# Block-sparse attention and a gated feed-forward layer on one core: four weight slices loaded and converted in halves, all operations in another order

## The chip, the cores and the metric

The kernel runs on one core of one Trainium2 chip. The metric is the time of one execution on the device in microseconds (us). PE is TensorE (matrix products), DVE is VectorE, ACT is ScalarE, POOL is GpSimd and SP is SyncE, which here issues nearly all loads and stores. Each engine has one queue of instructions and works through it in order.

## The reference

The inputs are q, k and v (4 batches, 8 heads, 768 positions, 64 wide) and two weight matrices, w_in (512 x 2048) and w_out (2048 x 512), all float32. Attention is local and blockwise, and its result goes through a layer with a cosine gate.

```python
def _attn_ref(q, k, v):
    B, H, S, D = q.shape
    block, window = (32, 16)
    nb = S // block
    k_sum = k.reshape(B, H, nb, block, D).max(axis=3)
    v_sum = v.reshape(B, H, nb, block, D).mean(axis=3)
    scores_l = scale * np.matmul(q, k.transpose(0, 1, 3, 2))
    mask_l = np.abs(pos[:, None] - pos[None, :]) < window
    scores_s = scale * np.einsum('bhsd,bhnd->bhsn', q, k_sum) + np.log(block)
    scores_l_m = np.where(mask_l, scores_l, -1000000000.0)
    a = softmax(np.concatenate([scores_l_m, scores_s], axis=-1))
    return np.matmul(a, np.concatenate([v, v_sum], axis=2))

def _moe_ref(x, w_in, w_out):
    h = x @ w_in
    return (h * np.cos(h)) @ w_out
```

The attention's output, heads side by side, is x (3072 x 512).

## The kernel before, in words

The 3072 rows of x are cut into eight blocks of 384 rows (half a batch each). A block has four groups, a to d, of two heads. a0 is group a of block 0, d7 group d of block 7. For each group the kernel loads q, k and v, turns q and k so that the head's width lies on the partitions, takes the maxima of k over blocks of 32, makes the scores, the exponentials and the normalized weights, turns those, and multiplies by v and the block means of v. The group's 128 columns of x are kept as a high part and a low part (xh, xl), so that products in a faster format lose nothing.

The feed-forward layer is cut into 16 slices of 128 columns of w_in and 128 rows of w_out. w0 to w15 are the slices. A step is one block with one slice. There are 128 of them, s0 to s127: s0 to s5 are block 0 with slices 0 to 5, s6 to s21 block 1 with all 16, s22 to s31 block 0 with slices 6 to 15, and from s32 on each block has 16. A step is twelve products that make h (`up`, L738), five operations on ACT, DVE or POOL that make the gate and its two parts (`tu`, `re`, `si`, `ga`, `hi`, `lo`: L748, L751, L756, L760, L383 or L385, L389), and nine products that add to the block's output (`dh` and `dl`, L789).

A slice is loaded by two DMAs (L404 for w_in, L408 for w_out), shifted by some bytes. ACT takes a byte of each element apart (`ab`, L417) and makes bits of it (`sh`, L422); DVE joins them with the rest (`fb`, L429); the result is split into a high part (`hi`, L383 on ACT or L385 on DVE) and a low part (`lo`, L389). Each of these handles 128 x 1024 elements: 512 columns of w_in's part and 512 of w_out's.

The order of everything is written out by hand in ORDER (L32), a text of tokens such as `w1.ab.1` (slice 1, operation ab, into buffer 1) or `s1.up.0` (step 1, the up products, into PSUM bank 0). The last letter of a token may name the engine: a is ACT, v is DVE, p is POOL. The program emits instructions in this order, so each engine's queue, and SP's queue of DMAs, has the order of the tokens that belong to it; semaphores follow from the data. FILL (L22) names tokens ahead of which PE is given products of zeros (L960), and how many. The tokens of attention are q, k, v and m (loads at L468, L468, L489 with L497, and L504; m brings the block means to where the group reads them), tk and tq (turns on PE, L532 and L519), ck and cq (copies, L383 or L385 and L525 or L527), ks (maxima, L551), ms (masks as a product, L571), sc (scores, L593), mx (L610), ex (L626), sm (L635), iv (L638), nm (POOL, L641), tp (turns, L650), cp (copies), va (the product with the values, L694), xh and xl (L383 or L385, L389). For batch 0 the block means of v come from `v0_0` and `v0_1`: l is the load (L906), vm six products (L914), ve the copies. For later batches POOL or DVE sums v (`v1_0` to `v3_7`, `s`, L254).

## Time and profile before

| what | value |
|---|---|
| three runs | 634.01, 634.37, 636.49 us (median 634.37) |
| the profiled execution | 635.47 us, its span 633.6 us |
| granted clock of TensorE, mean | 1.00 |
| PE busy | 620.6 us |
| DVE busy | 426.8 us |
| ACT busy | 315.7 us |
| POOL busy | 208.7 us |
| HBM read and written | 54.43 MB and 16.52 MB |

The span is the time from the first to the last instruction. An engine's busy time is the sum of its instructions' times, overlaps counted once. A row in order of time has the start, the length, the engine, the line, what is written and read, the shape and the count; the brackets behind it give how long the engine had been idle ahead of it and what ended that. A row with a count above one is merged from instructions that follow each other, and its length is that of all of them.

### The profile page before, as it was taken

The page shows a single profiled execution, that of the slowest core. Times are in us where ns is not written, and L with a number is a line of the kernel's source. Part 1 is how long each engine was busy: PE and PEld are TensorE (multiplying, and loading weights), DVE is VectorE, ACT ScalarE, POOL GpSimd, SP SyncE. Part 2 cuts the span into 40 slices and gives each one's busy share as a digit, 9 for nine tenths or more (in the row PEclk, how much of TensorE's full clock was granted, in tenths as well). Part 3 has the DMA queues.
Part 4 walks back from the last instruction along what each step waited for, and adds up shares of the span by engine and source line. Part 5 has one row for each costly group of instructions (what it writes and reads, how often), then busy time and mean ns, then how long its engine had stood idle before and what let it go on. Part 6 is the DMA issues. An engine that isn't in the chain of part 4 may idle for free.

```text
span 633.6 us, 12128 instructions
## 1 busy us (share of the span) xinstructions
PE 620.6 (98%) x4596; PEld 546.6 (86%) x4596; DVE 426.8 (67%) x795; ACT 315.7 (50%) x557; POOL 208.7 (33%) x243
## 2 busy tenths in 40 slices
...
GB/s 218 289 235 203 283 238 187 164 80 109 104 157 123 100 152 117 110 87 115 77 128 98 134 109 109 72 78 62 72 116 87 100 47 98 93 25 34 17 1 50
DMA packets 171305, 74.10 MB, mean 117 GB/s; under 512 B 136944, under 2 KB 160112, under 8 KB 171248
## 3 DMA queue, kind: packets, MB, share of 16 engines
...
q10 hardware_dynamic: 144, 0.13, 0.1%
HBM read 54.43 MB, written 16.52 MB: 112 GB/s over the span
## 4 chain that ended last, share of the span: by engine, by line
PE 91%; SPq 3%; DVE 2%; DMA 2%; ACT 1%; POOL 0%; issue 0%; DVEq 0%; ACTq 0%
PE banks L738 41%; PE banks L789 41%; PE banks L694 4%; PE banks L581 3%; DMA late<-in_moe_w_out_dram 2%; SPq L468 2%; PE banks L650 1%; PE banks L593 0%; ACT L756 0%; SPq L497 0%; SPq L906 0%; SPq L489 0%; ACT t L756 0%; DVE t L760 0%; DVE xl L389 0%
## 5 line engine op out<-in xcount | busy, mean ns | idle before, releaser
L738 PE MATMUL banks<-xh,w 128*128 128x384 f32 x1024 | 267.0, 337 | 0.0
L789 PE MATMUL banks<-w,gh 128*128 128x512 f32 x768 | 197.4, 392 | 0.6 <-DVE stage L827 0.6
L738 PEld LDWEIGHTS banks<-xh,w 128*128 128x128 f32 x1024 | 185.3, 188 | 2.4 <-issue 1.3
L738 PE MATMUL banks<-xl,w 128*128 128x384 f32 x512 | 171.1, 334 | 0.0
L789 PEld LDWEIGHTS banks<-w,gh 128*128 128x128 f32 x768 | 142.7, 188 | 31.4 <-issue 1.2
L389 POOL TENSOR_TENSOR gl<-t,gh 128x384 fp32r<-128x384 f32 x67 | 68.7, 1029 | 240.2 <-DVE gh L385 84.6
L748 ACT ACTIVATE t<-banks 128x384 int32<-128x384 f32 x128 | 62.3, 489 | 162.4 <-PE banks L738 88.0
L751 DVE SCALAR_TENSOR_TENSOR t<-t,banks 128x384 f32<-128x384 int32 x128 | 69.7, 547 | 66.7 <-ACT t L748 66.3
L789 PE MATMUL banks<-w,gl 128*128 128x512 f32 x384 | 108.7, 391 | 0.0
L760 DVE TENSOR_TENSOR t<-t,banks 128x384 f32<-128x384 f32 x128 | 69.6, 548 | 41.9 <-ACT t L756 40.2
L756 ACT ACTIVATE t<-t 128x384 f32<-128x384 f32 x128 | 66.3, 523 | 63.0 <-DVE t L751 62.7
L738 PEld LDWEIGHTS banks<-xl,w 128*128 128x128 f32 x512 | 96.1, 188 | 0.3
L789 PEld LDWEIGHTS banks<-w,gl 128*128 128x128 f32 x384 | 71.8, 188 | 15.3 <-issue 0.2
L641 POOL TENSOR_TENSOR sc<-sc,r 128x720 f32<-128x720 f32 x28 | 40.1, 1432 | 58.6 <-DVE r L638 54.5
L383 ACT CAST gh<-t 128x384 fp32r<-128x384 f32 x62 | 31.4, 510 | 35.3 <-DVE t L760 19.2
L617 POOL TENSOR_TENSOR sc<-sc,m 128x720 f32<-128x720 f32 x24 | 34.0, 1415 | 44.5 <-DVE m L614 41.3
L389 DVE TENSOR_TENSOR gl<-t,gh 128x384 fp32r<-128x384 f32 x61 | 38.9, 640 | 11.5 <-ACT gh L383 6.6
L385 DVE CAST gh<-t 128x384 fp32r<-128x384 f32 x66 | 25.3, 383 | 15.8 <-PE banks L789 12.5
L254 POOL TENSOR_TENSOR kn<-kn 96x256 f32<-96x256 f32 (+1 forms) x38 | 25.7, 677 | 23.7 <-DMA kn<-in_v_dram 22.0
L601 DVE SCALAR_TENSOR_TENSOR sc<-banks,mask 128x360 f32<-128x360 f32 x48 | 24.2, 519 | 13.4 <-PE banks L581 13.4
L635 DVE TENSOR_REDUCE r<-sc 128x6 f32<-128x726 f32 x28 | 25.1, 897 | 10.0 <-ACT sc L631 9.6
L664 DVE STREAM_TRANSPOSE stage<-sc 128x768 f32<-128x768 f32 x24 | 23.3, 970 | 10.5 <-POOL sc L641 10.2
(115 smaller groups left out, 558.0 us busy)
## 6 DMA issues: line engine op xcount, KB each, us to landing
pd<-stage SPq DMA_DIRECT2D x24, 384.0 KB
late<-in_moe_w_out_dram SPq DMA_DIRECT2D x16, 511.6 KB
late<-in_moe_w_in_dram SPq DMA_DIRECT2D x16, 510.5 KB
pt<-pd SPq DMA_DIRECT2D x72, 96.0 KB
vn<-in_v_dram SPq DMA_DIRECT2D x50, 120.0 KB
...
kn<-in_v_dram SPq DMA_DIRECT2D x24, 192.0 KB
...
```

Source lines behind the costliest of these rows:

```text
L254: eng.tensor_tensor(out=t[:, :n], in0=t[:, :n], in1=t[:, n:], op=ALU.add)
L383: eng.copy(out=out, in_=in_)
L389: eng.tensor_tensor(out=lo, in0=src, in1=hi.bitcast(F32), op=ALU.subtract)
L617: nc.gpsimd.tensor_tensor(out=self.sc, in0=self.sc, in1=self.m.unsqueeze(2).broadcast_to([P, U, NK]), op=ALU.subtract)
L641: nc.gpsimd.tensor_tensor(out=self.sc, in0=self.sc, in1=self.r.unsqueeze(2).broadcast_to([P, U, NK]), op=ALU.mult)
L694: nc.tensor.matmul(out=self.xps[rows, t * QT : (t + 1) * QT], lhsT=self.vn[:, t, rows], rhs=self.pt[2 * c + hh][s], start=True, stop=True,)
L738: nc.tensor.matmul(out=self.h, lhsT=w_of(name, self.f)[:, c * P : (c + 1) * P], rhs=x_of(self.blk, part, c), start=n == 0, stop=n == last,)
L748: nc.scalar.activation(out=self.t.bitcast(I32), in_=self.h, func=AF.Copy, scale=1.0 / TWO_PI, bias=0.25)
L751: nc.vector.scalar_tensor_tensor(out=self.t, in0=self.t.bitcast(I32), scalar=-TWO_PI, in1=self.h, op0=ALU.mult, op1=ALU.add)
L756: nc.scalar.activation(out=self.t, in_=self.t, func=AF.Sin, scale=-1.0, bias=-0.5 * math.pi)
L760: nc.vector.tensor_tensor(out=self.t, in0=self.t, in1=self.h, op=ALU.mult)
L789: nc.tensor.matmul(out=self.acc[i], lhsT=g[:, i * P : (i + 1) * P], rhs=w_of(name, self.f), start=self.first and n == 0, stop=self.last an ...
```

## The change

Slices 1, 0, 2 and 5 are loaded and converted in two halves. Half 0 is w_in's part, half 1 is w_out's. A token such as `w1.l.0` loads one half, and `ab`, `sh`, `fb`, `hi` and `lo` take the half as a first argument; the other twelve slices go on whole. The conversion's class gets a dictionary of its pieces for this. ORDER is another text: nearly every operation of the whole program stands at another place, with other PSUM banks, and some operations are on other engines (low parts of steps are 57 times on POOL, where before has 67, and 71 times on DVE, where before has 61). The last tokens, from s127.dl on, are as before. FILL has 66 products of zeros, where before has 56, at other tokens. The diff, with ORDER cut to its first part:

```diff
-FILL = {"a0.tk.1": 15, "a0.tk.0": 2, "b0.tq": 8, "c0.tk.0": 2, "b0.tk.0": 2, "d0.tk.0": 2, "b0.tk.1": 3, "c0.tp.0": 9, "b1.ms": 4, "b1.tq": 3, "a1.ms": 3, "a0.va": 3}
+FILL = {"a0.tk.1": 18, "a0.tq": 5, "b0.tk.0": 8, "c0.tq": 5, "d0.tk.1": 3, "d0.ms": 10, "b1.ms": 5, "a0.va": 12}
...
 ORDER = """
-a0.k a0.tk.1.0 a0.ck.1.a a0.ks.1 a0.ms.7.6 a0.tk.0.5 a0.ck.0.a b0.q a0.q a0.tq.4 a0.cq.v a0.ks.0 a0.sc b0.tq.0 c0.k
-c0.tk.0.1 a0.mx a0.ex d0.k b0.k b0.tk.0.2 b0.ck.0.a c0.ks.0 d0.tk.0.3 d0.tk.1.4 d0.ck.1.v c0.tk.1.5 c0.ck.1.a
-c0.ck.0.a b0.ms.6.7 b0.tk.1.1 b0.ks.0 a0.sm d0.ks.1 a0.iv a0.nm v0_0.l c0.q c0.tq.2 c0.cq.a d0.q d0.tq.4 c0.ks.1
-c0.ms.5.2 c0.sc b0.ks.1 b0.ck.1.a b0.cq.v b0.sc d0.cq.v c0.mx w1.l a0.tp.1.0 a0.tp.0.1 w1.ab.1 w1.sh c0.ex a0.cp.1.a
-w1.fb d0.ck.0.v c0.sm w1.hi.v d0.ks.0 w1.lo.v v0_0.vm.4 v0_1.l v0_1.vm v0_1.ve.a c0.iv b0.mx a0.cp.0.v d0.ms.0.5 d0.sc
-d0.mx c0.v w0.l w0.ab.1 w0.sh w0.fb w0.hi.v w0.lo.v b0.ex a0.v c0.nm c0.tp.0.4 b1.ms.1.2 b1.q b1.tq.3 a1.ms.6.7
-b1.cq.a c0.tp.1.3 b1.sc d0.ex d0.sm d0.iv b0.sm w2.l w2.ab.1 w2.sh w2.fb w2.hi.v b0.iv a0.m c0.m a0.va.0 c0.cp.0.a
-c0.cp.1.a d0.m a1.q a0.xh.a a1.tq.5 a1.cq.a d0.nm d0.tp.1.4 c0.va.3 c0.xh.a d0.tp.0.5 d0.cp.0.a w2.lo.v w5.l w5.ab.1
-d0.cp.1.a w5.sh a0.xl c0.xl a1.sc a1.mx a1.ex c1.ms.5.0 c1.q c1.tq.3 c1.cq.v b0.nm b0.tp.0.4 w5.fb d0.v d0.va.3
-b0.cp.0.a c1.sc d1.q d1.tq.6 d0.xh.a d1.cq.a d1.ms.4.7 b0.tp.1.6 b0.cp.1.a d1.sc a1.sm a1.iv c1.mx c1.ex a1.nm b0.m
-d0.xl b1.mx b0.v b0.va.3 b0.xh.a b0.xl w5.hi.v w5.lo.p b1.ex a1.tp.1.6 a1.tp.0.5 a1.cp.1.a c1.sm b1.sm c1.iv s1.up.0
-s1.tu a1.cp.0.v s1.re d1.mx w4.l w4.ab.0 w4.sh w4.fb w4.hi.v w4.lo.v s0.up.1 s0.tu s2.up.2 s5.up.3 w3.l w3.ab.1 w3.sh
...
+a0.k a0.tk.1.0 a0.ks.1 a0.ck.1.a b0.q a0.q a0.tk.0.7 a0.tq.6 a0.cq.a a0.ks.0 a0.ms.0.1 a0.ck.0.v a0.sc c0.k b0.k
+b0.tk.0.2 b0.tq.3 b0.tk.1.4 c0.tk.1.5 w1.l.0 c0.q d0.k c0.tk.0.6 b0.ck.1.a c0.ck.1.a c0.tq.7 c0.ck.0.a w1.ab.0.1
+c0.cq.a a0.mx b0.ks.0 v0_0.l v0_1.l b0.cq.a a0.ex w1.sh.0 c0.ks.1 b0.ks.1 b0.ck.0.v c0.ms.5.4 d0.tk.1.7 c0.ks.0 c0.sc
+c0.mx c0.ex d0.tk.0.6 b0.ms.0.1 b0.sc v0_0.vm.2 w1.fb.0 a0.sm d0.ck.0.v a0.iv w1.hi.0.v w1.lo.0.p c0.sm b0.mx c0.iv
+w1.l.1 w1.ab.1.1 w1.sh.1 w1.fb.1 w1.hi.1.v b0.ex w1.lo.1.v v0_1.vm v0_1.ve.a b1.q d0.q b1.tq.5 d0.tq.4 d0.ms.3.0
+d0.ks.0 d0.ck.1.v d0.cq.v d0.ks.1 w0.l.0 w0.ab.0.1 w0.sh.0 w0.fb.0 w0.hi.0.v w0.lo.0.v w0.l.1 w0.ab.1.1 w0.sh.1 c0.v
+d0.sc b1.cq.a d0.mx d0.ex w0.fb.1 w0.hi.1.v w0.lo.1.v c0.nm a0.nm a0.tp.1.7 a0.tp.0.6 c0.tp.1.1 c0.tp.0.2 b1.ms.4.5
+b1.sc d0.sm a1.ms.0.3 w2.l.0 w2.ab.0.1 w2.sh.0 w2.fb.0 w2.hi.0.v a0.cp.0.a a0.cp.1.a c1.q a0.v d0.iv d0.nm w2.lo.0.v
+w2.l.1 w2.ab.1.1 a0.m a0.va.6 c0.cp.1.a c0.cp.0.a b0.sm b0.iv a1.q a1.tq.7 a1.cq.v a0.xh.a a0.xl w2.sh.1 w2.fb.1
+c1.tq.1 d0.tp.1.2 a1.sc c1.cq.a c0.m c0.va.6 d0.cp.1.a a1.mx a1.ex d0.tp.0.7 d0.cp.0.a c1.ms.1.2 c1.sc b0.nm w2.hi.1.v
+w5.l.0 w2.lo.1.p w5.ab.0.1 c0.xh.v c0.xl b0.tp.1.6 d0.v d1.q d1.tq.0 d1.cq.a b0.m d0.m d0.va.3 w5.sh.0 b0.cp.1.a
+b0.tp.0.7 b0.cp.0.a d1.ms.0.6 a1.sm c1.mx c1.ex b1.mx b1.ex w5.fb.0 w5.hi.0.v b0.v b0.va.7 b0.xh.v b0.xl a1.iv d1.sc
+w5.l.1 w5.lo.0.p w5.ab.1.1 w5.sh.1 d0.xh.v d0.xl s1.up.1 a1.nm a1.tp.0.7 a1.tp.1.2 s1.tu a1.cp.0.a a1.cp.1.a w4.l
+w4.ab.0 w4.sh s5.up.5 s0.up.7 s2.up.2 c1.sm w5.fb.1 c1.iv c1.nm c1.tp.1.3 c1.tp.0.4 b1.sm s1.re w5.hi.1.v d1.mx b1.iv
+d1.ex w4.fb w4.hi.v w4.lo.v w3.l w5.lo.1.p w3.ab.1 s0.tu s0.re w3.sh w3.fb w3.hi.v w3.lo.v a1.m a1.v a1.va.0 c1.cp.1.a
+c1.cp.0.a s4.up.6 s0.si s0.ga s1.si s1.ga s0.hi.a s0.lo.v v1_0.l c1.v d1.m c1.m c1.va.3 c1.xh.a c1.xl s1.hi.a s2.tu
+s3.up.4 s1.lo.v a1.xh.a s3.tu d1.sm s2.re s3.re s2.si s2.ga s0.dh.7.1.3 s2.hi.v s0.dl s1.dh s1.dl s2.dh d1.iv s3.si
+s3.ga s3.hi.a s3.lo.v s4.tu s2.lo.v s2.dl b1.nm v1_0.s.p v1_1.l v1_1.s.p w8.l d1.v b1.m s4.re d1.nm d1.tp.0.2
...


         def __init__(self, f, raw):
-            self.f, self.raw = f, raw.bitcast(I32)
-
-        def load(self):
+            self.f, self.raw, self.u = f, raw.bitcast(I32), {}
+
+        def span(self, *h):
+            return slice(h[0] * DM, (h[0] + 1) * DM) if h else slice(0, 2 * DM)
+
+        def load(self, *h):
             f, t, n = self.f, self.raw.bitcast(U8), 8 * P
-            nc.sync.dma_start(
-                out=t[:, : NC * n].rearrange("p (c n) -> p c n", c=NC)[:, :, : n - CUT],
-                in_=w_in8.rearrange("(c p) n -> p c n", p=P)[:, :, n * f + CUT : n * (f + 1)],
+            if h != (1,):
+                nc.sync.dma_start(
+                    out=t[:, : NC * n].rearrange("p (c n) -> p c n", c=NC)[:, :, : n - CUT],
+                    in_=w_in8.rearrange("(c p) n -> p c n", p=P)[:, :, n * f + CUT : n * (f + 1)],
+                )
+            if h != (0,):
+                nc.sync.dma_start(
+                    out=t[:, NC * n : 2 * NC * n - CUT], in_=w_out8[f * P : (f + 1) * P, CUT :]
+                )
+
+        def apart(self, *args):
+            *h, i = args
+            self.u[tuple(h)] = room_for(i)[:, self.span(*h)]
+            byte = self.raw.bitcast(I8).rearrange("p (n b) -> p n b", b=8)[:, self.span(*h), 4]
+            nc.scalar.activation(
+                out=self.u[tuple(h)].bitcast(F32), in_=byte, func=AF.Prelu, scale=1.0, bias=EDGE, alpha=STEEP
             )
-            nc.sync.dma_start(
-                out=t[:, NC * n : 2 * NC * n - CUT], in_=w_out8[f * P : (f + 1) * P, CUT :]
-            )
-
-
-
-        def apart(self, i):
-            self.u = room_for(i)
-            byte = self.raw.bitcast(I8).rearrange("p (n b) -> p n b", b=8)[:, :, 4]
+
+        def first_bits(self, *h):
             nc.scalar.activation(
-                out=self.u.bitcast(F32), in_=byte, func=AF.Prelu, scale=1.0, bias=EDGE, alpha=STEEP
-            )
-
-        def first_bits(self):
-            nc.scalar.activation(
-                out=self.u, in_=self.u.bitcast(F32), func=AF.Prelu, scale=2.0 ** 27, bias=-(2.0 ** 28) * EDGE,
+                out=self.u[h], in_=self.u[h].bitcast(F32), func=AF.Prelu, scale=2.0 ** 27, bias=-(2.0 ** 28) * EDGE,
                 alpha=1.0 / STEEP,
             )

-        def join(self):
-            rest = self.raw.rearrange("p (n two) -> p n two", two=2)[:, :, 0]
+        def join(self, *h):
+            rest = self.raw.rearrange("p (n two) -> p n two", two=2)[:, self.span(*h), 0]
             nc.vector.scalar_tensor_tensor(
-                out=self.u, in0=rest, scalar=5, in1=self.u, op0=ALU.logical_shift_right, op1=ALU.bitwise_or,
+                out=self.u[h], in0=rest, scalar=5, in1=self.u[h], op0=ALU.logical_shift_right, op1=ALU.bitwise_or,
             )
-            self.uf = self.u.bitcast(F32)
-
-        def high_part(self, eng):
-            wm[self.f] = wp.tile([P, 4 * DM], F32R, name=f"w{self.f}", tag=f"w{self.f}")
-            copy(eng, wm[self.f][:, : 2 * DM], self.uf)
-
-        def low_part(self, eng):
-            rest(eng, wm[self.f][:, 2 * DM :], self.uf, wm[self.f][:, : 2 * DM])
+
+        def high_part(self, *args):
+            *h, eng = args
+            if self.f not in wm:
+                wm[self.f] = wp.tile([P, 4 * DM], F32R, name=f"w{self.f}", tag=f"w{self.f}")
+            copy(eng, wm[self.f][:, self.span(*h)], self.u[tuple(h)].bitcast(F32))
+
+        def low_part(self, *args):
+            *h, eng = args
+            low = wm[self.f][:, 2 * DM :][:, self.span(*h)]
+            rest(eng, low, self.u[tuple(h)].bitcast(F32), wm[self.f][:, self.span(*h)])


     class Group:

```

More of the change, by code (lines that the diff above doesn't have):

```diff
@@ new lines @@
+s58.ga s58.hi.v s58.lo.v s62.tu s62.re s58.dh s58.dl s60.hi.a s59.dh s59.dl s62.si s60.lo.p s61.tu s61.re s62.ga
+s61.si s61.ga s61.hi.v c4.po a5.pt.0 c5.q c4.pi c4.va.1 b5.sc.2.6 s61.lo.p s63.tu c4.xh.v s60.dh s60.dl s63.re
+s62.hi.v c5.qt b5.z.0.v s63.si s63.ga s62.lo.v b5.z.1.v s61.dh s61.dl s63.hi.a s62.dh s62.dl s63.lo.p s63.dh s63.dl
+d4.po v3_7.l d4.pi d4.v c5.kw.a c5.sc.2.3 c4.xl d4.m d4.va.1 d4.xh.a d4.xl v3_7.s.v s65.up.6 s65.tu s65.re s65.si
+b5.mx c5.z.1.v s65.ga d5.q a5.po b5.su s63.ta.0.0.a b5.ex b5.sm s65.hi.v a6.k a6.kt.0 a6.kt.1 b5.iv s65.lo.p d5.qt
@@ new lines @@
+d5.mx c5.iv s73.up.5 s71.up.3 s72.up.0 s69.hi.a s73.tu s73.re s69.lo.p s71.tu s71.re s71.si s69.dh b5.po b5.v c6.k
+b5.m c5.nm c5.pt.1 d5.su s71.ga s73.si s73.ga a6.qt b6.ks.0 a6.kw.v s71.hi.v s69.dl s70.dh s71.lo.p s70.dl s71.dh
+s71.dl c6.kt.0 a6.sc.1.3 a6.z.0.v d5.ex d5.sm d5.iv b6.kw.a s72.tu s73.hi.a s73.lo.p d5.nm b5.pi b5.va.5 b5.xh.a
+a5.xh.v a6.z.1.v a6.mx a5.xl s72.re b6.q s75.up.1 s74.up.3 c5.po d5.pt.1 s72.si s72.ga b5.xl s76.up.6 s77.up.0 c5.v
+c5.pi c5.m c5.va.5 b6.qt s72.hi.v s72.dh c6.kt.1 s72.lo.v s72.dl s76.tu s76.re s73.dh s73.dl s76.si s74.tu s74.re
```

237 lines of the change are left out of this document (112 added, 125 removed).

## Prediction

> **What bounds the kernel now.** I read the page first, then a table of stretches, then the order in time of the first 48 us.
>
> ```profile
> span 633.6 us, 12128 instructions
> PE 620.6 (98%) x4596; PEld 546.6 (86%) x4596; DVE 426.8 (67%) x795; ACT 315.7 (50%) x557; POOL 208.7 (33%) x243
> PE 91%; SPq 3%; DVE 2%; DMA 2%; ACT 1%; POOL 0%; issue 0%; DVEq 0%; ACTq 0%
> ...
> 0.00:7.66 7.66, 5.63 (x28) 3.78 (x29) 4.15 (x22) 2.25 (x3) 5.44 (x37) 1.00 0.79 178
> 7.66:34.04 26.38, 22.34 (x343) 15.06 (x344) 17.87 (x31) 14.66 (x40) 2.78 (x2) 1.00 0.99 270
> 34.04:47.47 13.43, 11.57 (x271) 9.10 (x271) 11.85 (x20) 11.68 (x29) 5.11 (x3) 1.00 0.83 242
> 47.47:160.00 112.53, 112.53 (x740) 101.61 (x739) 96.44 (x159) 76.24 (x128) 56.83 (x57) 1.00 0.64 181
> 160.00:200.00 40.00, 39.30 (x311) 33.82 (x310) 27.98 (x53) 17.10 (x28) 17.85 (x24) 1.00 0.48 126
> 200.00:618.00 418.00, 418.00 (x2862) 374.33 (x2861) 261.85 (x502) 188.83 (x321) 120.50 (x122) 1.00 0.34 87
> 618.00:633.60 15.60, 11.20 (x50) 8.94 (x48) 6.61 (x13) 4.95 (x10) 0.20 (x1) 0.99 0.14 50
> ```
>
> The columns of the stretches are the bounds, the length, the busy time of PE, its weight loads, DVE, ACT and POOL, then the granted clock, the DMA share and GB/s. PE has work for 620.6 of 633.6 us. Its 13 us of rest are 2.03 + 4.04 + 1.86 before 47.47 us, 0.70 between 160 and 200, and 4.40 at the end, where the last step drains; the order of the last tokens is the same in both kernels. The work of PE that counts is also the same: the same products, the same 128 steps. So only two things can move: PE's rest with the products of zeros that fill it, nearly all before 47.47 us, and new rest later, where there is now almost none. DMA is 99% busy from 7.66 to 34.04: the start is held by loads.
>
> **How large the prize is.** The fills are 56 products of zeros before and 66 after.
>
> ```profile
> 1.05 3.38 PE L960 MATMUL banks<-part_sum 128*128 128x256 bf16 x15 [1.05 <-DVE part_sum L279]
> 4.38 0.88 PE L532 MATMUL banks<-ident,late 128*128 128x128 f32 x3
> 27.51 1.16 PE L960 MATMUL banks<-part_sum 128*128 128x256 bf16 x9
> 28.51 0.60 PE L650 MATMUL banks<-ident,late 128*120 128x128 f32 x4
> 46.87 0.87 PE L650 MATMUL banks<-ident,sc 128*120 128x128 f32 x6
> 47.50 0.42 PE L738 MATMUL banks<-xh,w 128*128 128x384 f32 x1
> ```
>
> The first 15 take 3.38 us, 0.225 us each, at a PE not yet at speed; nine later ones take 28.51 - 27.51 = 1.00 us, 0.11 each. Fills cost 3.38 + 41 x 0.11 = 7.9 us before and 18 x 0.225 + 48 x 0.11 = 9.3 us after, as far as they don't lie in waits. The first product of the steps (s1.up, L738) starts at 47.50. In the new order the six turns of a1 (L650, 47.50 - 46.87 = 0.63 us) come behind s1.up instead of ahead of it; all else that precedes it is the same set. So the mark to beat is 47.47 - 0.63 = 46.84. Real work ahead of that mark is 39.54 busy - 7.9 - 0.63 = 31.0 us. The new order therefore can't reach s1.up before 1.05 + 9.3 + 31.0 = 41.4: the gain is at most 5.5 us, and only with PE never waiting.
>
> **Loads.** What lands when?
>
> ```profile
> late<-in_moe_w_in_dram SPq DMA_DIRECT2D x8, 510.5 KB
> late<-in_moe_w_out_dram SPq DMA_DIRECT2D x7, 511.6 KB
> late<-in_v_dram SPq DMA_DIRECT2D x4, 384.0 KB
> late<-in_q_dram SPq DMA_DIRECT2D x12, 96.0 KB
> late<-in_v_dram SPq DMA_DIRECT2D x8, 120.0 KB
> late<-in_k_dram SPq DMA_DIRECT2D x4, 192.0 KB
> late<-in_v_dram SPq DMA_DIRECT2D x4, 40.0 KB
> ...
> 13.74 0.96 SPq L408 DMA_DIRECT2D late<-in_moe_w_out_dram  x1
> 18.95 1.14 ACT L417 ACTIVATE stage<-late 128x1024 f32<-128x1024 int8 x1 [2.18 <-DMA late<-in_moe_w_out_dram]
> 23.42 2.73 PE L914 MATMUL banks<-late,early 128*24 128x512 f32 x6 [1.21 <-DMA late<-in_v_dram]
> 27.85 1.15 ACT L417 ACTIVATE stage<-late 128x1024 f32<-128x1024 int8 x1 [0.93 <-DMA late<-in_moe_w_out_dram]
> ```
>
> A k (two issues) is 0.384 MB, a q 0.192, half of the v for the block means 0.768, a group's v 0.28, a slice 1.022, half a slice 0.511. Up to w1 the queue of before holds 4.09 MB, which landed at 18.95; up to the second v0 4.86 MB, at 23.4; up to w0 6.16 MB, at 27.85. That is near 245 GB/s from about 2 us on, plus one to two us. By that, estimated from these three rows, the new order has w1.0 (2.05 MB) at 12, v0_1 (4.16) at 20, w1.1 (4.67) at 22, w0.0 (5.57) at 25, w0.1 (6.08) at 27, w2.0 (6.87) at 30, w2.1 (7.85) at 34, the means of a0 (a0.m, 7.9, issued behind w2.1) at 34, b0's v (9.6) at 40.5, where before had 10.1 MB ahead of the end of b0's v, since w5 was loaded whole ahead of it. So the halves bring the x inputs forward by 0.5 MB, about 2 us, and nothing more: SP's queue stays in order, and the bytes are the same.
>
> **The walk.**
>
> ```profile
> 26.50 1.09 PE L593 MATMUL banks<-kd,late 64*64 64x96 f32 x48
> 29.38 0.47 PE L571 MATMUL banks<-band,turned 98*128 98x360 bf16 x2
> 34.04 0.92 PE L694 MATMUL banks<-pt,vn 120*64 120x64 f32 x24
> 36.30 0.44 PE L650 MATMUL banks<-ident,late 128*120 128x128 f32 x2 [0.87 <-DMA late<-in_moe_w_out_dram]
> 46.02 0.92 PE L694 MATMUL banks<-pt,early 120*64 120x64 f32 x24
> ...
> 29.99 1.60 ACT L626 ACTIVATE sc<-banks,m 128x120 f32<-128x120 f32 x6
> 34.86 1.39 POOL L641 TENSOR_TENSOR late<-late,r 128x720 f32<-128x720 f32 x1 [7.32 <-DVE r L638]
> 21.20 1.23 DVE L429 SCALAR_TENSOR_TENSOR stage<-late,stage 128x1024 int32<-128x1024 int32 x1 [0.99 <-ACT stage L422]
> 23.62 0.68 DVE L385 CAST w<-stage 128x1024 fp32r<-128x1024 f32 x1
> 24.69 1.21 DVE L389 TENSOR_TENSOR w<-stage,w 128x1024 fp32r<-128x1024 f32 x1
> 45.20 0.55 DVE L389 TENSOR_TENSOR xl<-banks,xh 128x384 fp32r<-128x384 f32 x1
> ```
>
> First the start. Three more cold fills (0.7 us) and five more in front of a0's q delay the first turns, but a0.sc waits for q and its copies and stays near 7.7 us: nothing, covered by the q load.
>
> Then the way to the first product with the values, a0.va, which before has at 34.04. It needs a0.m, w2.1 being just ahead of it in SP's queue: about 34 again. On the way there is a new head-of-line wait: DVE has w1.fb.1, w1.hi.1 and w1.lo.1 ahead of d0.ks.0, d0.ck.1 and d0.cq, and w1.fb.1 needs w1.1 (22) and two passes on ACT, half of 1.14 each (23.2). DVE then does about 0.6 + 0.4 + 0.6, half of the rows at 21.20, 23.62 and 24.69, and four operations of the shape of the row at 45.20 (0.55) for d0, so d0.sc starts at about 27, and PE rests up to 2 us just behind its ten fills. From there PE has two scores (27.51 - 26.50 = 1.0 each), twelve turns (1.3), two sets of masks (up to 0.47 each) and 17 fills (1.9): 6 us, ready at 33. Loads and PE nearly meet there. Value taken for a0.va: 34.0, between 32.5 (d0.sc not held up) and 36 (w1.1 and a0.m 2 us later).
>
> Then the way from a0.va to s1.up. The set of PE operations is that of before less a1's turns. Before needed 13.43 us, of which 1.86 was rest: the longest, 0.87 at 36.30, is put down to a DMA, but the row of POOL's normalizing (34.86 + 1.39 = 36.25) is what ended it, since ACT had held d0's exponential behind whole slices. Without rest 11.57 - 0.63 = 10.9 us. In the new order d0.nm comes earlier in the list, but b0.cp and with it b0.va stand on ACT behind a1.ex (1.60), w5.ab.0, d1.cq and w5.sh.0; worked along ACT from a1.mx at 38 (1.6, then eight copies and half passes of 0.4 to 0.6), b0.va starts at 42.9 and s1.up, with 0.85 and d1's 1.0 between, at 44.8. Extra hand-offs of halves: I take 0.4. So 45.2, a gain of 46.84 - 45.2 = 1.6 us. Bounds: -0.5 (a0.va at 36) to +3.3 (a0.va at 32.5 and no rest).
>
> What the halving itself costs lies in this too. One DVE row gives 1.21 us for 1024 elements, another 0.55 for 384: 1.03 ns per element and 0.15 us that each instruction pays anyhow, 22% of a half's 0.68. Nine more instructions on DVE (four joins, four high parts, one low part) make 1.4 us, 1.1 of it ahead of s1.up, where DVE rests 47.47 - 4.15 - 17.87 - 11.85 = 13.6 us. It counts only through the waits above; a third of it is the 0.4. [...]
>
> Last what follows s1.up.
>
> ```profile
> 47.47:60.00 12.53, 12.53 (x95) 12.25 (x94) 12.11 (x16) 10.61 (x22) 7.49 (x5) 1.00 0.74 195
> ```
>
> Between 47.47 and 160 PE has no rest, with DVE busy for 96.44 of 112.53. The new list of DVE from s1.up to the first step of the next block has 45 instructions where before has 38 (b0.sm and c1.sm slip past, s2, s4 and s5 have their high parts on DVE). Walked along, DVE hands over s0, s2 and the last xl with 0 to 1 us to spare. I take 0.7 us of new rest, bounds -0.7 (the rest at 160 goes too) to +4. From 200 us on the order is another, with the same kinds of operations and DVE at 63%: nothing, bounds 0 to 1.5.
>
> **Sum.** -1.6 + 0.7 = -0.9 us: a span of 632.7. The profiled execution took 635.47, 1.87 more than its span, and 1.1 more than the median of 634.37; the difference is carried to the median: 633.5.
>
> **The rivals.**
> DVE takes over behind s1.up (slower). The place: s5, w9 and the last xl. b1.xl and d1.xl, which s7.up needs, are queued on DVE behind w9.fb and w9.hi; w9's load stands in SP's queue behind a load that waits for POOL's sums. My walk has w9 landing near 66 and s7.up due at 77, and DVE with 1 us to spare. Each microsecond that DVE's list is longer than that is a microsecond of PE; from 5 us on it is slower by over 0.5%. It would be 634.37 - 1.6 + 5.5 = 638.3. For: DVE at 12.11 of 12.53 between 47 and 60 us and 18% more instructions. Against: 112 us without any rest of PE so far.
> The change doesn't do what it says. Loads come by bytes; the half of w1 lands with nobody needing it, DVE's wait for w1.1 costs 2 us ahead of d0.sc, a0.va comes at 35.6, and the gain is gone: 634.4. For: 99% DMA up to 34 us. Against: b0's v is ahead of half of w5.
> The start is free of waits (faster). Here a0.va comes at 32.5, with no rest to s1.up: -3.3 and the 0.7 us at 160 gone: 630.4. Against it: PE would have to run nearly dense from 8 us on, where before rested for 4.04 of 26.4.
> [...]
>
> **How the numbers follow.** About 0.5% (3.2 us: 631.2 and 637.5) is what a measurement of this kernel can tell from no change. Forecast 0.52 (632 to 635), no gain 0.20, free start 0.14, DVE 0.09, clock 0.05. Faster takes most of the free start, 0.13; slower the DVE rival and little of the clock, 0.10; the rest, 0.77, is the same. The range leaves out the far ends of the free start and of DVE: 630.8 to 636.6.
>
> **What would show it.** Right: a0.va near 34, s1.up between 44.5 and 46, rest ahead of d0.sc with DVE's kd copy or L429 as its end, w1.lo.1 done only after 24. Wrong: s1.up before 43.5 or after 47; more than 2 us of PE rest between s1.up and 160; any granted clock under 1.00 ahead of 40 us; rest of PE over 1.5 us between 200 and 618.

## The result, and the profile after

The changed kernel takes 642.45 us (median of 4 runs, 639.69 to 643.5) where the kernel before, on the same chip, takes 635.0 (634.01 to 636.49): a ratio of 1.0113, 95% interval 1.0083 to 1.0143. It is slower, by 1.1%. The forecast was no change, 633.5 us, and its range ended at 636.6. The profiled execution took 642.63 us, its span 640.9.

First three lines of the page of the changed kernel, then a table of stretches with the columns as before: bounds, length, busy time of PE, weight loads, DVE, ACT and POOL, granted clock, DMA share, GB/s.

```profile
span 640.9 us, 12178 instructions
PE 624.6 (97%) x4606; PEld 547.4 (85%) x4606; DVE 430.4 (67%) x813; ACT 318.0 (50%) x565; POOL 205.7 (32%) x237
PE 84%; DVE 5%; ACT 5%; issue 2%; DMA 2%; SPq 2%; POOL 0%; DVEq 0%; POOLq 0%; ACTq 0%
```

```profile
10.00:20.00 10.00, 6.49 (x129) 5.26 (x128) 6.93 (x14) 6.31 (x19) 1.09 (x1) 1.00 1.06 307
20.00:30.00 10.00, 10.00 (x69) 3.98 (x71) 6.30 (x12) 4.72 (x14) 3.40 (x3) 0.83 0.92 251
30.00:40.00 10.00, 7.95 (x139) 6.10 (x130) 8.10 (x16) 7.26 (x18) 2.83 (x2) 1.00 0.90 234
40.00:48.55 8.55, 8.30 (x234) 6.97 (x233) 7.91 (x16) 7.43 (x24) 2.21 (x3) 1.00 1.00 316
48.55:60.00 11.45, 11.45 (x96) 11.12 (x89) 11.19 (x18) 10.16 (x23) 9.54 (x8) 1.00 0.36 83
60.00:160.00 100.00, 95.86 (x576) 83.54 (x575) 82.93 (x130) 61.37 (x95) 50.95 (x52) 1.00 0.63 172
160.00:200.00 40.00, 40.00 (x317) 34.98 (x316) 31.30 (x62) 25.23 (x42) 18.86 (x25) 1.00 0.51 142
200.00:618.00 418.00, 418.00 (x2902) 373.97 (x2901) 262.33 (x514) 186.31 (x318) 109.35 (x110) 1.00 0.34 88
```

Two stretches lose the time. One is the start. s1.up (its first product) comes at 48.58 us instead of 47.50. Since the 0.63 us of a1's turns now stand behind it, that is 1.7 us behind the mark of the prediction. The other is 60 to 160 us, where PE rests 100 - 95.86 = 4.14 us; before, it had no rest from 47.47 to 160 and 0.70 us behind that. From 160 to 618 PE never rests. Measured to the last product of all (636.17 after, 628.81 before), the loss is 7.36 us: 1.08 up to s1.up and 6.29 behind it, 0.63 of which are the turns. Of the other 5.7 us, 3.4 are more rest of PE (4.14 against 0.70). For the remaining 2.2 us PE is busy longer with the same products: 583.5 us from s1.up on with the turns, 580.6 before without them. What makes it so, no run here settles.

**The start.** PE's rows in order of time, with the idle time ahead of them and what ended it in the brackets, and then ACT's:

```profile
19.91 0.32 PE L603 MATMUL banks<-kd,late 64*64 64x96 f32 x3 [2.58 <-issue]
20.16 7.03 PE L924 MATMUL banks<-late,early 128*24 128x512 f32 x12
...
29.32 1.09 PE L603 MATMUL banks<-kd,late 64*64 64x96 f32 x48
...
32.89 0.70 PE L970 MATMUL banks<-part_sum 128*128 128x256 bf16 x5 [1.03 <-ACT late L535]
...
36.27 1.47 PE L970 MATMUL banks<-part_sum 128*128 128x256 bf16 x12 [0.93 <-ACT pt L386]
37.67 0.92 PE L704 MATMUL banks<-pt,vn 120*64 120x64 f32 x24
```

```profile
31.12 0.69 ACT L424 ACTIVATE stage<-late 128x512 f32<-128x512 int8 x1 [1.95 <-DVE w L392]
...
37.69 0.70 ACT L424 ACTIVATE stage<-late 128x512 f32<-128x512 int8 x1 [1.20 <-DVE w L392]
```

At 17.3 us PE stops in the middle of b0.sc, three of its products short, for 2.58 us, and "issue" says that it waited for nothing that the profile shows. Then the twelve products for the block means take 7.03 us, where before two groups of six took about 2.7 us each. Later ACT rests twice ahead of `ab`, the byte of a slice's second half, until DVE has finished the low part of the first half. These are the second halves of w0 and w2, which use the stage buffer of their first halves. What ACT has behind the first of them comes late for PE: b1.cq (L535), which ends PE's rest at 32.89, and further on a0.cp (L386). ACT's second rest ends at 37.69, when a0.va has begun, and so doesn't hold it. a0.va is at 37.67, 3.7 us later than predicted.

**The clock.** Two stretches of 3.41 us from the same kernel: the one that holds the rest, and the next.

```profile
17.50:20.91 3.41, 1.00 (x5) 0.44 (x5) 3.21 (x8) 0.26 (x2) 1.27 (x1) 1.00 1.10 312
20.91:24.32 3.41, 3.41 (x5) 0.65 (x4) 1.95 (x2) 2.80 (x8) 3.23 (x2) 0.50 0.97 309
```

The clock is 0.50 from 20.91 to 24.32 us, right behind a stretch in which PE was busy for 1.00 of 3.41 us. In e1_buffers below, at full clock, the twelve products take 5.33 us instead of 7.03: the half clock costs 1.7 us.

**Behind s1.up.** Two of the rests, each with the rows of POOL, DVE and PE that belong to it:

```profile
70.72 1.64 POOL L257 TENSOR_TENSOR kn<-kn 96x256 f32<-96x256 f32 x2
70.16 1.89 DVE L392 TENSOR_TENSOR gl<-t,gh 128x384 fp32r<-128x384 f32 x2 [0.64 <-ACT gh L386]
72.10 0.97 PE L799 MATMUL banks<-w,gl 128*128 128x512 f32 x3 [1.37 <-DVE gl L392]
...
115.04 2.40 POOL L392 TENSOR_TENSOR w<-stage,w 128x1024 fp32r<-128x1024 f32 x1 [4.30 <-ACT w L386]
115.50 2.36 DVE L392 TENSOR_TENSOR gl<-t,gh 128x384 fp32r<-128x384 f32 x1 [1.61 <-PE banks L799]
121.32 1.66 PE L799 MATMUL banks<-w,gh 128*128 128x512 f32 x6 [1.83 <-ACT gh L386]
```

The low part of a step (`lo`, tile gl) takes DVE about 0.55 us. At 115.50 it took 2.36 and ended 0.42 us behind POOL's low part of w10, which had begun 0.46 us earlier. So it took 1.8 us longer than usual and was done only behind POOL's: these two rows read as DVE held by POOL, and in e2_lo_dve below, with w10's low part off POOL, it takes 0.56 us again. The other rest shown, at 70 us, is longer in this execution than in others: e1_shift, e1_less_fill, e1_buffers and e2_lo_dve below have the same order there and 0.44 to 0.46 us in place of 1.37.

### The profile page after: what moved, and what is told of

Same layout as the page of the kernel before. It is cut to its first block, busy times and chain, and to the rows that moved or that the text cites. A ratio compares the mean times of both kernels' runs of the same rounds, so it can differ in the third digit from the quotient of the medians.

```text
span 640.9 us, 12178 instructions
## 1 busy us (share of the span) xinstructions
PE 624.6 (97%) x4606; PEld 547.4 (85%) x4606; DVE 430.4 (67%) x813; ACT 318.0 (50%) x565; POOL 205.7 (32%) x237
## 4 chain that ended last, share of the span: by engine, by line
PE 84%; DVE 5%; ACT 5%; issue 2%; DMA 2%; SPq 2%; POOL 0%; DVEq 0%; POOLq 0%; ACTq 0%
PE banks L799 37%; PE banks L748 37%; PE banks L704 4%; PE banks L591 3%; DVE stage L436 1%; ACT stage L424 1%; ACT stage L429 1%; PE banks L924 1%; DVE w L392 1%; SPq L478 1%; DVE w L388 1%; DMA late<-in_q_dram 1%; PE banks L603 1%; DMA vn<-vs 1%; DVE t L770 0%
## 5 line engine op out<-in xcount | busy, mean ns | idle before, releaser
L392 POOL TENSOR_TENSOR gl<-t,gh 128x384 fp32r<-128x384 f32 x57 | 59.1, 1037 | 253.8 <-PE banks L799 124.7
L392 DVE TENSOR_TENSOR gl<-t,gh 128x384 fp32r<-128x384 f32 x71 | 45.1, 637 | 15.1 <-ACT gh L386 6.7
L386 ACT CAST gh<-t 128x384 fp32r<-128x384 f32 x60 | 30.5, 512 | 40.1 <-DVE t L770 22.6
L388 DVE CAST gh<-t 128x384 fp32r<-128x384 f32 x68 | 27.1, 398 | 21.6 <-PE banks L799 19.3
L257 POOL TENSOR_TENSOR kn<-kn 96x256 f32<-96x256 f32 (+1 forms) x38 | 28.8, 757 | 25.2 <-DMA kn<-in_v_dram 23.6
```

The costliest lines, as they stand in the source:

```text
L257: eng.tensor_tensor(out=t[:, :n], in0=t[:, :n], in1=t[:, n:], op=ALU.add)
L386: eng.copy(out=out, in_=in_)
L388: eng.tensor_copy(out=out, in_=in_)
L392: eng.tensor_tensor(out=lo, in0=src, in1=hi.bitcast(F32), op=ALU.subtract)
```

## The experiments

The theories were these. For the start: PE waits for its own instructions, which come by DMA behind the loads, and the clock falls after that; the shared stage buffer delays ACT. The rival: the halving itself, with more and smaller operations, costs the time. For the stretch behind s1.up: DVE is held by POOL; the rival: the new order feeds the steps too late, whatever POOL does; a second rival: the new start leaves work undone that comes due later. In the table "to the end" is from s1.up's first product to the last product of the kernel, which leaves out the final stores (from the last product to the end of the span it is 4.7 us in the changed kernel and 5.9 in e2_halves_before). The ratios are to the kernel before as timed together with each run.

| run | median us | ratio to before, 95% interval | a0.va | s1.up | to the end | half clock ahead of 160 us |
|---|---|---|---|---|---|---|
| before (five times; profile) | 634.7 to 635.5 | 1 | 34.04 | 47.50 | 581.31 | none |
| after | 642.45 | 1.0113 [1.0083, 1.0143] | 37.67 | 48.58 | 587.60 | 3.41 us at 20.9 |
| e1_shift | 639.68 | 1.0063 [1.0036, 1.0091] | 35.74 | 46.64 | 586.45 | 3.41 at 28.8 |
| e1_less_fill | 643.6 | 1.0137 [1.0097, 1.0177] | 34.39 | 48.46 | 588.20 | 6.83 at 35.6, 3.41 at 120.9 |
| e1_buffers | 639.77 | 1.0085 [1.0057, 1.0113] | 33.97 | 44.91 | 586.97 | none |
| e1_whole | 643.8 | 1.0139 [1.0105, 1.0173] | 36.35 | 49.90 | 586.83 | 3.41 at 15.9 |
| e2_lo_dve | 639.85 | 1.0076 [1.0050, 1.0102] | 37.31 | 48.23 | 585.81 | 3.41 at 20.8 |
| e2_halves_before | 637.62 | 1.0042 [1.0023, 1.0062] | 32.04 | 48.12 | 581.79 | 3.41 at 40.7 |
| e2_buffers_lo | 638.85 | 1.0052 [1.0023, 1.0080] | 34.19 | 45.10 | 586.12 | none |
| e2_all | 638.32 | 1.0056 [1.0041, 1.0071] | 33.80 | 44.70 | 585.03 | none |
| e3_tail_before | 641.64 | 1.0092 [1.0073, 1.0110] | 35.54 | 46.46 | 588.29 | 3.41 at 19.9 and at 60.9 |
| e3_tail_shift | 641.53 | 1.0093 [1.0074, 1.0112] | 34.56 | 45.68 | 590.04 | 3.41 at 27.9, 6.83 at 58.6 |
| e3_head_before | 640.3 | 1.0072 [1.0052, 1.0093] | 33.92 | 47.69 | 586.37 | 3.41 at 16.7 |
| e4_handover | 638.22 | 1.0042 [1.0027, 1.0058] | 35.43 | 46.34 | 584.46 | 3.41 at 20.1 |
| e4_handover_fill | 635.89 | 1.0013 [0.9997, 1.0028] | 34.52 | 45.42 | 583.53 | none |

The columns from a0.va on are from one profiled execution each; whether the clock falls differs between executions of the same kernel (the four of the changed kernel have mean clocks of 0.996, 0.999, 0.997 and 0.997).

### e1_shift: fewer products of zeros ahead of b0.sc

```diff
-FILL = {"a0.tk.1": 18, "a0.tq": 5, "b0.tk.0": 8, "c0.tq": 5, ...
+FILL = {"a0.tk.1": 18, "c0.tq": 5, ...
```

> The new kernel without the 13 products of zeros ahead of a0's q turns and b0's first k turns, so that 26 PE instructions fewer stand ahead of b0's scores. Code theory: the 2.6 us rest of PE at 17.3 us, with three of b0's scores left, is PE waiting for its next block of instructions, whose fetch (it lands at 18.6 us) was queued behind loads. Then the rest leaves b0's scores and shows, if at all, 13 instruction pairs later, inside the block-mean products; it is under 1.3 us, the granted clock stays at 1.00 up to 40 us, the twelve block-mean products take 5.5 us in place of 7.0, s1.up starts 1.5 to 2.5 us earlier than 48.6 and the time falls by about 2 us, to 640.4. Rival (b0's scores waited for data or a bank): the rest stays where it is in the order, ahead of the last three of b0's scores, 2 us or longer.

PE's instructions come in blocks over the DMA queue that the page lists as "instruction": 36 packets of 16 KB for 2 x 4606 products and weight loads, by that quotient 256 in each. In the changed kernel PE entered a block at 9.82 us, counted back 256 from the rest, and the next one was fetched only from 17.64 to 18.60, while loads took 1.06 of the DMA engines' time between 10 and 20 us (a packet counts whole where it starts, so a share can pass 1). PE had by then used up its block in the middle of b0.sc. With 13 products of zeros fewer ahead of it the boundary lies later: the fetch ended at 19.26, the block was entered only at 21.72, and the rest of 2.58 us is gone. That part of the theory holds, and not in this pair alone: in all eight runs with the new start and these zeros PE rests ahead of the same product, for 0.8 to 2.6 us, and goes on 1.1 to 1.6 us after the fetch has ended; in the four without them (e1_shift, e2_all, e3_tail_shift, e4_handover_fill) that rest is missing. But the gain is 1.9 us at s1.up and no more, since d0.sc, which waits for DVE (d0.cq, L537), then leaves PE a rest of 1.58 us at 25.4, and the clock falls behind that one instead:

```profile
21.72 1.45 PE L924 MATMUL banks<-late,early 128*24 128x512 f32 x3
...
26.95 0.29 PE L603 MATMUL banks<-kd,late 64*64 64x96 f32 x1 [1.58 <-DVE late L537]
```

### e1_less_fill: no products of zeros ahead of b1.ms and a0.va

```diff
-... "d0.ms": 10, "b1.ms": 5, "a0.va": 12}
+... "d0.ms": 10}
```

> The new kernel without the 5 products of zeros ahead of b1's masks and the 12 ahead of a0's values product. Theory that fills stand on the path: they write the PSUM bank of the operation that follows and so begin only when that bank is free, when the operation could begin itself. Then a0.va starts 1.3 to 1.9 us earlier than 37.67 and s1.up up to 1.5 us earlier than 48.58; time about 641. Rival (the values product waits for its loads and copies anyway): a0.va stays within 0.4 us of 37.67.

Stretches of this run: the one ahead of the fall, and two later ones.

```profile
32.16:35.57 3.41, 1.83 (x43) 1.37 (x34) 2.89 (x6) 2.36 (x6) 0.28 (x1) 1.00 1.01 260
...
35.00:44.00 9.00, 8.08 (x149) 6.70 (x144) 6.46 (x14) 5.33 (x15) 4.34 (x3) 0.62 0.86 247
118.00:126.00 8.00, 6.17 (x21) 4.61 (x20) 6.60 (x13) 5.77 (x10) 4.67 (x3) 0.79 0.74 154
```

The fills do delay PE, but by less than a0.va shows, which comes 3.3 us earlier. 2.2 us of that lie ahead of d0.sc (27.16 against 29.32), where this execution had no half clock at 20 us and a shorter rest in b0.sc (1.79 us). From d0.sc to a0.va it is 7.23 us against 8.35: 1.1 us are the fills'. All of it is lost again at s1.up, as the clock then falls for 6.83 us behind a stretch with 1.83 us of work. It falls once more at 120.9, behind the rest of 1.83 us that the changed kernel has at this place, too, without such a fall. Here the fills keep the clock up: the changed kernel, with them, has 1.00 from 30 to 48.55 us.

### e1_buffers: the second halves in the other stage buffer

```diff
-w1.ab.1.1 ... w0.ab.1.1 ... w2.ab.1.1
+w1.ab.1.0 ... w0.ab.1.0 ... w2.ab.1.0
```

> The new kernel with the second halves of w1, w0 and w2 taken apart into the other stage buffer. Theory that halves queue on one buffer: ACT stands 1.95 us at 31.1 and 1.2 us at 37.7 us until DVE has made the first half's low part, and b1.cq and a0.cp behind it are late. Then both waits of ACT go, PE's rests at 32.9 (1.03) and 36.3 (0.93) shrink by 1 to 1.9 us together, and s1.up comes 1 to 2 us earlier: 640 to 641. Rival (ACT waits for the loads): the waits of ACT stay, only their releaser changes to a DMA, and the time stays within 0.7 us of 642.4.

```profile
10.00:20.00 10.00, 7.84 (x134) 5.95 (x135) 6.84 (x14) 6.31 (x19) 1.00 (x1) 1.00 1.05 310
20.00:30.00 10.00, 10.00 (x95) 5.81 (x94) 8.61 (x16) 7.22 (x21) 3.45 (x3) 1.00 1.03 300
30.00:44.88 14.88, 13.80 (x330) 10.86 (x327) 13.41 (x27) 12.12 (x36) 5.08 (x4) 1.00 0.74 194
...
60.00:160.00 100.00, 96.42 (x599) 84.13 (x599) 82.86 (x133) 61.39 (x96) 52.94 (x56) 1.00 0.62 175
```

```profile
26.61 1.43 PE L603 MATMUL banks<-kd,late 64*64 64x96 f32 x48
...
33.97 0.92 PE L704 MATMUL banks<-pt,vn 120*64 120x64 f32 x24
```

Here the start has the times that were predicted: a0.va at 33.97 (34.0 predicted), s1.up at 44.91 (45.2). Not all of that is the buffer's. From d0.sc to a0.va it is 7.36 us against 8.35, so that the buffer is worth 1.0 us; the other 2.7 us lie ahead of d0.sc (26.61 against 29.32). The rest in b0.sc is still there, but shorter in this execution, 1.49 us, and falls so that the clock stays up; others of this kernel, with mean clocks of 0.991 to 0.997, took up to 5 us more. And behind s1.up nothing has changed: 3.58 us of rest between 60 and 160. A start that is 3.7 us earlier than in the changed kernel saves 2.7 in the median, part of it by the clock: with a mean clock of 0.998 or more, executions take 637.95 to 638.33 here and 639.69 in the changed kernel. It doesn't reach the kernel before.

### e1_whole: the new order, no halves

```diff
-w1.l.0 ... w1.l.1 w1.ab.1.1 ...
+w1.l ... w1.ab.1 ...
```

> The new order with w1, w0, w2 and w5 loaded and converted whole: loads at the place of the first half's load, conversions of w1, w0 and w2 at the place of the second half's, of w5 at the first half's. Rival theory that halving itself is the loss: the time falls to that of before, 634 to 636. Order theory: the halves cost under 1 us of it, the stalls behind s1.up (4 to 5 us between 60 and 145 us of the span, where DVE and POOL overlap) stay, and the time is 640 to 645.

Slices 1, 0, 2 and 5 whole, loaded where the first half was, give 643.8 us. PE now rests 2.59 us at 11.9, since a load of q stands behind a whole w1, and s1.up comes at 49.90. So in the new order the halves are worth 1.3 us at s1.up, and the rival that they are the loss falls, for this order.

### e2_halves_before: the order of before, with halves

```diff
-w1.l ... w1.ab.1 w1.sh ... w1.fb ... w1.hi.v ... w1.lo.v
+w1.l.0 w1.l.1 ... w1.ab.0.1 w1.ab.1.0 w1.sh.0 w1.sh.1 ... w1.fb.0 w1.fb.1 ... w1.hi.0.v w1.hi.1.v ... w1.lo.0.v w1.lo.1.v
```

> The order, the fills and the PSUM banks of the kernel before, with w1, w0 and w2 converted in halves at the places where they stood whole (the two loads of a slice are the same two as before; the second half is taken apart into the other stage buffer). Theory that the order and not the halving is the loss: within 1.5 us of before, clock 1.00 up to the end's drain. Rival that the split's extra instructions cost: slower by 2 us or more.

Slices 1, 0 and 2 are halved in place, everything else is as before. It is slower, 637.62 us. a0.va comes 2.0 us earlier than before, but s1.up 0.6 us later. What turns the one into the other is in these rows, first of this run, then of before:

```profile
36.09 2.44 DVE L391 TENSOR_TENSOR w<-stage,w 128x512 fp32r<-128x512 f32 x2
36.25 1.73 POOL L650 TENSOR_TENSOR sc<-sc,r 128x720 f32<-128x720 f32 x1 [2.00 <-DVE r L647]
39.05 0.31 PE L580 MATMUL banks<-band,turned 98*128 98x360 bf16 x1 [1.61 <-DVE xl L391]
```

```profile
38.09 1.22 DVE L389 TENSOR_TENSOR w<-stage,w 128x1024 fp32r<-128x1024 f32 x1
38.24 2.33 POOL L641 TENSOR_TENSOR sc<-sc,r 128x720 f32<-128x720 f32 x1 [1.99 <-DVE r L638]
```

Before, DVE began w2's low part 0.15 us ahead of POOL's normalizing, and POOL was the one to wait (2.33 us instead of 1.39). In two halves POOL gets in between them, and DVE waits: 2.44 us for the two instead of 2 x 0.69. A queue with a0.xl and c0.xl in it is late, PE rests 1.61 us, and the clock is at half from 40.7 on. Here the halving does cost, by what it lets in between. The sizes don't meet, though: to its last product the profiled execution loses 1.1 us to that of before, while the medians differ by 2.4.

### e2_lo_dve: the low part of w10 on DVE

```diff
-w10.lo.p
+w10.lo.v
```

> The new kernel with one change: w10's low part on DVE in place of POOL. Theory of the shared access of DVE and POOL: POOL's 2.40 us instruction at 115.04 held DVE's low part of a step, which took 2.36 us from 115.50 in place of 0.55, and PE's longest rest behind s1.up (2.0 us near 119) came of it. Then DVE's low part takes under 0.8 us, its new w10 row 1.2 to 1.3 us, the 2.0 us rest near 119 shrinks by 1 us or more, and the time falls by 1 to 2 us to 641. Rival (DVE's queue is too long there, whoever holds it): DVE gets 1.2 us more work, the rest stays at 2 us or grows.

```profile
114.22 0.56 DVE L392 TENSOR_TENSOR gl<-t,gh 128x384 fp32r<-128x384 f32 x1 [1.64 <-PE banks L799]
119.38 1.66 PE L799 MATMUL banks<-w,gh 128*128 128x512 f32 x6 [1.17 <-ACT gh L386]
```

One letter, and the time from s1.up to the end falls by 1.8 us. 0.7 of it is at this place, and `lo` takes 0.56 us again. Another 0.9 is at 70 us, where nothing was changed and the rest differs between executions, so it isn't the letter's. But a rest of 1.17 us stays at the same place: DVE still waited 1.64 us for PE to release the buffer, and had turns of k and w10's low part to do ahead of the next step's gate. So both theories have a part there: POOL's hold makes about a third of the 1.83 us, and what remains is put down to the order.

### e2_buffers_lo and e2_all: the mended pieces together

```diff
 e1_buffers, and
-s10.lo.p ... w10.lo.p
+s10.lo.v ... w10.lo.v
 e2_all: and the FILL of e1_shift
```

> The new kernel with the second halves of w1, w0 and w2 in the other stage buffer, and the low parts of w10 and of step 10 on DVE. If the waits add up as read from the traces: s1.up near 44.9 us, no half clock ahead of the end, rests behind s1.up 2 us in place of 5: a span near 634.5 and a time near 636. If PE's rests behind s1.up only move (DVE as the bound there), the span stays at 636 to 637.

> As the kernel with buffers and low parts changed, and without the 13 products of zeros ahead of a0's q turns and b0's first k turns, which took the instruction fetch's rest out of b0's scores. If the fetch's rest is on the path: another 0.5 to 1.5 us less, a span near 633.5, the time of before within 1 us. If the missing products of zeros let the clock fall, a row of 3.4 us at half clock shows ahead of 45 us and the time is 1 to 2 us above that of the kernel with them.

They take 638.85 and 638.32 us, where 636 and less was expected. The pieces don't add up: s1.up is at 44.70 in e2_all, 2.8 us ahead of before, and still 585.03 us remain behind it, 3.7 more than before (3.1 without a1's turns). PE rests at 66, 93, 97 and 114 us, places that differ little from run to run. That speaks for the order there, and against any single hold.

### e3_tail_before, e3_tail_shift, e3_head_before: one order ahead of s1.up, the other behind

```diff
 e3_tail_before: ORDER of e1_buffers up to s1.up, then what is left in the order of before, banks renamed
 e3_tail_shift: the same with the FILL of e1_shift
 e3_head_before: ORDER of before up to s1.up, then what is left in the new order, banks renamed
```

> The new start (with the second halves in the other stage buffer) up to s1.up, and behind it the operations in the order of the kernel before, banks renamed to fit. If the 5.6 us lost behind s1.up come from the new order of what stands there (steps fed just in time, DVE waiting behind GpSimd), the time from s1.up to the end falls from 591.7 to 587-588 us, s1.up stays near 44.9 us, and the execution takes about 634 us, 1 us under the kernel before. If they come from the new start itself (what it leaves undone at s1.up: half of slice 5 and the weights of a1), the time from s1.up stays at 590-592 us and the execution at 637-639 us.

> The run with the old order behind s1.up, and also without the 13 products of zeros ahead of a0.tq and b0.tk.0, which moves the boundaries of TensorE's blocks of instructions. If the order behind s1.up is the loss, the sum of 44.7 us to s1.up (as with that fill before) and 587-588 us behind it gives a span of 632 and an execution of 633.5-634 us, steadier than without the change of the fill, since the rest in b0.sc at 17 us goes. If the start is the loss, 637-639 us.

> The start of the kernel before, slices whole, up to s1.up (47.5 us), and behind it the operations in the new order, banks renamed to fit. If the loss behind s1.up is in the new order there, the time from s1.up is 590-592 us where the kernel before has 586.1, and the execution takes 639.5-641.5 us. If it comes from what the new start leaves undone, the time from s1.up is 586-588 us and the execution 635-637 us.

First a stretch of e3_head_before, then two of e3_tail_before.

```profile
60.00:160.00 100.00, 97.06 (x604) 84.65 (x602) 82.23 (x131) 62.48 (x97) 50.34 (x55) 1.00 0.63 171
```

```profile
46.43:60.00 13.57, 10.44 (x89) 9.88 (x80) 9.55 (x17) 8.03 (x16) 5.68 (x6) 1.00 0.73 203
...
70.00:160.00 90.00, 89.91 (x590) 79.30 (x589) 75.59 (x123) 59.08 (x93) 42.16 (x44) 1.00 0.61 172
```

The new order behind the old start brings the rests back, 2.94 us between 60 and 160, and 586.37 us to the end where before has 581.31: 5.1 of the 5.7 us, with a start that leaves nothing undone. The old order behind the new start has next to none from 70 us on. So the rests from 70 to 142 us belong to the new order there, and not to the start. The medians of the two runs with the old order behind were a miss, though: their seam put c1.iv, which c1's weights wait for, on DVE behind slice 4 and half of slice 5, and c1.nm on POOL behind slice 5's low part, and PE rested 3.1 us ahead of 60 us, with half clock behind it.

### e4_handover, e4_handover_fill: the seam mended

```diff
-s1.tu a1.cp.1.a c1.sm a1.cp.0.v s1.re d1.mx w4.l ... w4.lo.v w5.fb.1 w5.hi.1.v w5.lo.1.p b1.sm c1.iv ... d1.ex c1.nm
+s1.tu a1.cp.1.a c1.sm c1.iv a1.cp.0.v s1.re d1.mx w5.fb.1 w5.hi.1.v w5.lo.1.v w4.l w4.ab.0 w4.sh d1.ex ... w4.lo.v b1.sm ... c1.nm
 e4_handover_fill: also
-FILL = {"a0.tk.1": 18, "a0.tq": 5, "b0.tk.0": 8, "c0.tq": 5, "d0.tk.1": 3, "d0.ms": 10, ...
+FILL = {"a0.tk.1": 18, "c0.tq": 5, "d0.tk.1": 3, "d0.ms": 18, ...
```

> The new start with the other stage buffer, the old order behind s1.up, and the handover between them mended: in the run of this kind before, TensorE rested 3.3 us at 55 us because c1.iv stood on DVE behind slice 5 and b1.sm, and c1.nm on GpSimd behind slice 5's low part. Here c1.sm and c1.iv come right behind s1.tu, slice 5's low part is on DVE, d1.ex is ahead of slice 3. If the new start's gain is real and the new order behind s1.up was the loss, s1.up is at 45-46 us, the rest at 55 us under 0.5 us, the time from s1.up 587-588 us and the execution 633.5-635.5 us, at or 1 us under the kernel before. If the start leaves too much undone for any order behind it, DVE is late again somewhere between 50 and 65 us, by 2 us or more, and the execution takes 637 us or more.

> The same with the boundaries of TensorE's blocks of instructions moved (no zeros ahead of a0.tq and b0.tk.0) and 8 more products of zeros ahead of d0.ms, into the rest of 1.8 us ahead of d0.sc at 24 us. If that rest and the one in b0.sc are what brings the half clock in, no clock below 1.00 shows ahead of 600 us, and the time is steadier than the other run's and 0.5 to 1.5 us lower: 633-634.5 us. If the zeros delay d0.sc, s1.up comes up to 1 us later and the time is the same.

The stretches of e4_handover_fill from s1.up on:

```profile
45.39:60.00 14.61, 13.85 (x108) 12.91 (x100) 13.77 (x21) 11.55 (x23) 5.76 (x6) 1.00 0.76 211
60.00:160.00 100.00, 99.85 (x643) 88.99 (x644) 84.35 (x143) 65.69 (x106) 49.42 (x52) 1.00 0.62 178
```

With the eight more zeros into the rest ahead of d0.sc and the boundary of the block moved, the clock was at 0.998 to 1.00 in all twelve executions, and the twelve lie within 635.03 and 637.45. e4_handover, without these, had a clock of 0.995 or 0.996 in six of seven and takes 2.3 us more; the profile shows the rest of 2.0 us in b0.sc and the half clock behind it. So those two rests together are what brings the clock down; which of them counts for more, the run can't tell, as it changes both. The clock isn't the whole of the 2.3 us either: the seventh execution of e4_handover had it at 1.0 and took 638.62. Both times lie above what was expected.

The version is level with the kernel before, not faster: 1.0013, interval 0.9997 to 1.0028. Its last product starts at 628.95 us against 628.81. s1.up comes 2.08 us earlier, but 0.63 us are a1's turns that follow, and another 0.76 + 0.15 us PE rests up to 160, since DVE is busy for 13.77 of 14.61 us: it has the second half of w5, c1.sm and b1.sm to do, which the old start had done by then. What is left to explain is 2.22 - 0.63 - 0.91 = 0.68 us, in which PE is busy longer with the same products; that is not settled. The second rival, that the new start owes work, thus holds for at most 2.22 - 0.63 = 1.6 us of the 5.7, and the order behind s1.up for the larger part.

## Why the prediction was wrong, point by point

The sum gave -0.9 us, and measured to the last product it is +7.36. Of the miss, 3.4 us lie ahead of s1.up (45.2 against 48.58) and 5.0 behind it (0.7 against 5.7).

- The way from a0.va to s1.up: right. Predicted were 10.9 us of work and 11.2 with hand-offs; the changed kernel needs 10.91, e1_buffers 10.94.
- a0.va at 34.0: wrong by 3.7 us for the changed kernel, which has 37.67. d0.sc is 2.3 us late there (29.32 against 27) by the fetch and the clock, and the way from it to a0.va takes 8.35 us instead of 7. That e1_buffers has 33.97 is in part luck: loads, which were to hold a0.va, came sooner than forecast (w1's second half at 20.6 instead of 22) and held nothing there, and 1.49 us of rest came from the fetch instead of DVE. The walk left out three things. It took ACT's `ab` as free to start when the half has landed, and didn't look at the stage buffer that the token names, which DVE holds until the first half's low part. It counted instructions as present, and didn't see that they come by DMA too (36 packets, which the page counts as a share of the same 16 engines), with DMA 99% busy by its own table. And it put the 17 fills into 6 us that were to end a microsecond ahead of the loads; in the runs the 12 ahead of a0.va begin only when a0.cp is done (36.27 in the changed kernel, behind a rest), and a0.va follows them 1.4 us later. They write to the bank of the operation behind them and so lie on the path.
- d0.sc near 27, held by DVE behind w1's second half: right where PE comes in time. In e1_shift it starts at 26.95, and DVE's copy (L537) ends a rest of 1.58 us; in e1_buffers it starts at 26.61 without a rest. In the changed kernel PE itself is late, by the fetch and the clock, and d0.sc starts at 29.32 with DVE done 0.7 us ahead of it.
- The clock: a chance of 0.05, and it fell. No run shows a length of rest that decides it: it fell behind a rest of 2.58 us in b0.sc and, in e1_shift, behind one of 1.58 us ahead of d0.sc, and stayed at 1.00 behind one of 1.89 us there in e2_all. One window of 3.41 us at half clock cost 1.7 us (7.03 for the twelve products, against 5.33 in e1_buffers).
- The halves: the sum took their cost as instructions on DVE. In the rows, a half costs what was read from the slope (`fb` 0.69 us against 0.68), and 44.91 lies between 44.8, the walk without extra hand-offs, and 45.2 with them, so that point is not decided. What was missed is that the place between two halves can be taken by POOL: in e2_halves_before the two take 2.44 us where the whole one took 1.22.
- After s1.up: this is the step that failed by most. Predicted 0.7 us, bounds -0.7 to +4; measured 6.29 - 0.63 = 5.7. The walk along DVE stopped at the first step of the next block and used each operation's usual time. It didn't check what POOL does at the same moment, and it ended at 77 us: of the two largest rests it passed over the one at 70 us and never reached the one at 119. In its place the runs show the order of what stands behind s1.up: 5.1 us with the old start, by more rest of PE and by PE being busy longer with the same products. POOL's hold of DVE is part of that; the larger part isn't traced to single operations. The rival "DVE takes over" had the right engine and, by luck, the size (5.5 us at its price), but the wrong place: none of the larger rests ends on w9 or on the last xl.
- From 200 us on nothing: right; PE is busy for 418.00 of 418.00 us in both.

Of what was named as proof against the forecast, three came true: s1.up after 47, more than 2 us of rest between s1.up and 160, and a clock under 1.00 ahead of 40 us.
